# Another way to split 64-bit weights, and another clock model in the planner, in a recurrence-plus-feed-forward kernel

## The chip, the cores and the metric

The kernel runs on one core of one Trainium2 chip. The metric is the device time of one execution in microseconds; the figure before is the median of three executions. The engines are called by the profile's names: PE (TensorE matmuls), PEld (TensorE weight loads), DVE (VectorE), ACT (ScalarE), POOL (GpSimd), SP (SyncE, which issues all DMAs here).

## The reference

The first half is a recurrence over 768 tokens for 4 batches of 8 heads of 40 channels; the second is a gated feed-forward layer with d_ff 1536 on its 3072 x 320 result:

```python
for t in range(S):
    y[:, :, t] = np.einsum('bhd,bhde->bhe', rt, state)
    Sa = np.einsum('bhde,bhe->bhd', state, at)
    state_decay = state * wt[:, :, None, :] - np.einsum('bhd,bhe->bhde', Sa, bt)
    state = state_decay + np.einsum('bhd,bhe->bhde', vt, kt)
...
a = x @ w_a
b = x @ w_b
return (a * b @ w_out).astype(np.float32)
```

The three weight matrices are handed over in 64-bit floating point; everything else is float32.

## The kernel before, in words

**The recurrence** is computed in 12 chunks of 64 tokens, each in two halves `c`. For each half `prep` (line 639) loads the inputs, forms running products with scans on DVE, scales B, K and A, and has PE form the score blocks. `lanes` (line 752) inverts triangular blocks for a group of one or two chunks, in many small DVE steps (tiles `Y`, `Yt`), `join` (807) and `merge` (846) put the blocks together with 32-wide matmuls, and `main` (906) carries the state: PE matmuls, with copies on ACT (`RH`, `SV`, `uT`, `SD`) and products on DVE (`G`, `X`, `ST`) in between. Chunk n+1 needs the state of chunk n. What `main` leaves goes to DRAM (`x_d`), and `pack` (1037) loads it back as the moving operand of the feed-forward layer (`XF`, `xk`).

**The feed-forward layer** is cut into 12 tiles of 128 columns of d_ff. `unit` (510) is one tile against one chunk (256 tokens, tile `ab`) or, in the last third, against two chunks (512 tokens, tiles `at` and `m`): 16 matmuls, a copy on ACT, a product on DVE, a split into high and low part on ACT and on DVE or POOL, and 6 or 12 matmuls into `po`. Tiles 0 to 4 are decoded early, and their units run between the chunks of the recurrence. Two more tiles are decoded around the end of the recurrence and the other five after it.

**Decoding.** Every tile has three pieces (of `wa` and `wb`, 120 partitions x 384, and of `wo`, 128 x 320), 36 pieces in all. `decode` (427) turns one piece, loaded as pairs of 32-bit words, into a high and a low float32 part. It is a list of steps, each with its engine, its planned time and what it reads and writes. There is one set of the temporaries `w_ex`, `w_mt`, `w_rs` (`NTMP` = 1, line 38) and two raw buffers `wraw`. The steps before: the exponent bits of the high word are masked out on DVE; ACT rescales them (a Relu with scale 8 and a bias tile); DVE shifts and masks the mantissa; ACT turns the low word into a float; DVE puts the sign to the exponent, then mantissa to exponent; ACT casts that into the high part; DVE multiplies the low word's float by the signed exponent; a subtraction and an addition (DVE in the first three pieces, POOL in the others) make the low part.

**The order.** Nothing is run in the order of the program text. All steps are given to a planner (`Plan`, line 114), which simulates the engines with the planned times that each step carries, picks at each point the step that can start first (those within `slack` of it by their priority `v`), and emits the instructions in that order; `InOrder` (62) holds every engine to it. So each planned time has a say in the order of all engines. `us` (410) and `act` (416) are the formulas of a DVE and an ACT step of n elements; a PE step has a literal time, and a `work`, which the class `Clock` (95) sums over stretches of time to decide whether PE is taken to run at its full or its slow clock; `switch` (161) is added when PE passes from one kind of block to another. In the decode steps, the priorities `wv`, `PV`, `LV`, `UV` and the others are constants at the head of the file.

```python
def us(n, fixed=0.16, each=0.00106):
    return fixed + each * n
...
def act(n):
    return us(n, 0.17, 0.00088)
```

Of the kernel before, what the change touches and what calls it, by code (L numbers as in the profile page):

```python
# [9 lines left out]
F32 = mybir.dt.float32  # L10
# [42 lines left out]

PV, PV1, LV, MV, UV, WV, WV1 = -2.63, 0.52, -0.08, -0.82, 1.93, -0.57, 0.99
# [40 lines left out]
class Clock:  # L95

    WINDOW, ENOUGH, SLOW = 3.413, 5100, 1.85

    def __init__(self):
        self.work = {}  # L100

    def full(self, t):
        return self.work.get(int(t / self.WINDOW) - 1, 0.0) >= self.ENOUGH

    def run(self, t, d, work):

        left = 1.0
        while left > 1e-9:
            k = int(t / self.WINDOW)
            d1 = d if self.full(t) else d * self.SLOW  # L110
            part = min(left, ((k + 1) * self.WINDOW - t + 1e-9) / d1)
            self.work[k] = self.work.get(k, 0.0) + part * work
            t += part * d1
            left -= part
        return t


class Plan:
# [9 lines left out]
    def op(self, eng, dur, fn, r=(), w=(), v=None, lat=0.07, need=None, free=(), mode=None, moved=0.0, work=0, port=False):  # L128
        o = Op()
        o.moved, o.work, o.port = moved, work, port or (eng == "POOL" and dur != 1.2)  # L130
        o.eng, o.dur, o.fn, o.lat, o.need, o.free, o.mode = eng, dur, fn, lat, need, free, mode
        o.v = self.v if v is None else v
        o.pairs = PAIRS.get(fn.__name__, 8 if work in (3840, 7680) else 0) if eng == "PE" else 0
# [12 lines left out]
        return o  # L146
# [14 lines left out]
    def run(self, slack=0.05, switch=0.13):  # L161
# [17 lines left out]
        while todo:  # L179
# [31 lines left out]
            if o.eng == "PE":  # L211
                if o.mode != last_mode:
                    d += switch
                last_mode = o.mode
                if CLK:
                    t = engines["PE"]
                    if self.filler and s - t > 0.4:

                        share = FILL if clock.full(t) else FILLC
                        nf = int(share * (s - t) / (0.09 if clock.full(t) else 0.17))  # L220
                        for _ in range(nf):
                            self.filler()
                            t = clock.run(t, 0.09, 384)
                        self.nfill = getattr(self, "nfill", 0) + nf
                        s = max(s, t)
# [107 lines left out]
def wkv_moe(ctx, tc, wd, ai, bk, rvf, vn, pin, rv, wa, wb, wo, out):  # L333
# [60 lines left out]
    bias = const.tile([P, 1], F32, name="bias")  # L394
    nc.gpsimd.memset(bias, -8.0 * 0x38000000)
# [31 lines left out]
    def decode(i, src, rows, ncol, dst_hi, dst_lo, split):  # L427
# [10 lines left out]
        if not WIDE:  # L438
# [6 lines left out]
        rf, f = rs.bitcast(F32), mt.bitcast(F32)  # L445
# [4 lines left out]
        yield "DVE", us(ncol), lambda: ts(  # L450
            out=ex, in0=high, scalar1=0x7FF00000, scalar2=None, op0=ALU.bitwise_and), (kr,), (K[0],), None
        yield "ACT", act(ncol), lambda: nc.scalar.activation(
            out=ex, in_=ex, func=AF.Relu, scale=8.0, bias=bias[:rows]), (), (K[0],), None
        yield "DVE", us(ncol), lambda: ts(
            out=mt, in0=high, scalar1=3, scalar2=0x007FFFF8, op0=ALU.logical_shift_left, op1=ALU.bitwise_and), (kr,), (K[1],), None
# [3 lines left out]
        yield "DVE", us(ncol), lambda: stt(  # L459
            out=ex, in0=high, scalar=-2147483648, in1=ex, op0=ALU.bitwise_and, op1=ALU.bitwise_or), (kr,), (K[0],), None  # L460
        yield "DVE", us(ncol), lambda: nc.vector.tensor_tensor(out=mt, in0=ex, in1=mt, op=ALU.bitwise_or), (K[0],), (K[1],), None
# [48 lines left out]
    def unit(xk, kx, w, slot, first, last, done, v, wide=False, quick=False):  # L510
# [29 lines left out]
        for j in range(2):  # L540
            pl.op("PE", 1.81 if wide else 0.95, lambda j=j: half(j), list(kx) + wk, [kab], v=v, work=3840 * scale, mode="r", lat=0.1)
# [16 lines left out]
        def second2():  # L558
            second()

        pl.op("PE", 1.77 if wide else 0.9, second2 if wide else second, km[1:3] + [("wt", slot, 2), ("wh", slot, 2)], kpo,
              v=v - 0.2, work=3840 * scale, mode="r", lat=0.1)
# [76 lines left out]
    def prep(n, c, v):  # L639
# [67 lines left out]
        pl.op("PE", 1.15, scores, [kBK, kA], need=ps, work=4096, mode="q", lat=0.1, w=[("sc", q), kAB, kTK])  # L707
# [27 lines left out]
        for k in range(2):  # L735
            ps = Banks(1)

            def nat(k=k, ps=ps):
                for m in range(4):
                    transp(bank(ps)[:, m * P:(m + 1) * P], BK[:, k * 4 + m].rearrange("p x t -> p (x t)"))  # L740

            def natc(k=k, ps=ps):
                nc.scalar.copy(out=BN[:, k * 4:(k + 1) * 4], in_=bank(ps).rearrange("p (m j e) -> p m j e", m=4, j=2)[..., 0:D])
            pl.op("PE", 0.42, nat, [kBK], need=ps, work=832, mode="t", lat=0.1, w=[("nt", q, k), (*kBN, k)])
            pl.op("ACT", act(320), natc, [("nt", q, k)], [(*kBN, k)], free=[(ps, 0)])
# [61 lines left out]
    def join(n, x, v):  # L807
# [11 lines left out]
        pl.op("PE", 2.55, xt, [("EO", place[n]), ("T3", x)], [("j1", n), "W4"], need=ps, work=3072, mode="h", lat=0.1)  # L819
# [15 lines left out]
        pl.op("PE", 1.15, t3, ["W4", ("TC", x)], [("j2", n), ("T3", x)], need=ps, work=1024, mode="h", lat=0.1)  # L835
# [6 lines left out]
        pl.op("PE", 2.3, tc_, ["W4", ("j2", n)], [("j3", n), ("TC", x)], need=ps2, work=2048, mode="h", lat=0.1)  # L842
# [3 lines left out]
    def merge(n, x, v):  # L846
# [25 lines left out]
        pl.op("PE", 1.15, l2a, kab + [("T3", x)], [("l3", n), "W4"], need=ps, work=1024, mode="h", lat=0.1)  # L872
# [13 lines left out]
        pl.op("PE", 1.15, l2b, ["W4", ("TC", x)], [("l4", n), kT[2]], need=ps, work=1024, mode="h", lat=0.1)  # L886
# [19 lines left out]
    def main(n, c, v):  # L906
# [32 lines left out]
        pl.op("PE", 1.05, r_, [kS, kV, kU], [("r", q), kRH], need=ps, work=2560, mode="c", lat=0.1)  # L939
# [15 lines left out]
        pl.op("PE", 1.1, u_, [kRH, *kT], [("u", q), kS, ("ut", 0), ("ut", 1)], need=ps, work=3328, mode="q", lat=0.1)  # L955
# [9 lines left out]
        if n < NS - 1:  # L965

            ps = Banks(1)

            def s_(ps=ps):
                for i in range(4):  # L970
                    for gq in range(2):
                        for j in range(2):
                            c0 = (i * 2 + gq) * D
                            mul(bank(ps)[hd(j), c0:c0 + D], BN[:, mi(gq, i), j], SV[:, gq, j, i])
            pl.op("PE", 0.75, s_, [kU, kS, kV], [("s", q), kST], need=ps, work=2560, mode="c", lat=0.1)
# [19 lines left out]
        pl.op("PE", 1.15, g_, [("ut", 0), ("ut", 1), kRV], [("gs", q), ("gm", 0), ("gm", 1)], need=ps, work=4096, mode="q", lat=0.1, v=v + 0.1)  # L995
# [17 lines left out]
        pl.op("PE", 1.6, y_, [("gm", 0), ("gm", 1), kU, kRV, kSD], [("y", q), ("x", 0)], need=ps, work=6144, mode="c", lat=0.1, v=v + 0.1)  # L1013
# [8 lines left out]
        if n < NS - 1:  # L1022
# [6 lines left out]
            pl.op("PE", 0.45, sd_, [kST], [("sd_", q), kSD], need=ps, work=832, mode="t", lat=0.1, v=v + 0.3)  # L1029
# [421 lines left out]
```

## Time and profile before

| | |
|---|---|
| three executions | 789.76, 791.24, 792.59 us; median 791.24 us |
| the profiled execution's own time | 793.49 us |
| its span, first to last instruction | 791.8 us |
| busy in the span | PE 693.2, PEld 627.2, DVE 581.8, ACT 403.4, POOL 182.8 us |
| mean granted clock of PE | 0.898 of full speed |

The profiled execution took 2.25 us more than the median of the three; 1.7 us of its time lie outside its span. The page gives busy time by engine, 40 slices of about 20 us, and the chain of work that ended last; the trace behind it gives the same for any stretch.

### The profile page before, as it was taken

What the parts mean: (1) busy time and instruction counts of PE and PEld (TensorE: products, weight loads), DVE (VectorE), ACT (ScalarE), POOL (GpSimd) and SP (SyncE); (2) the same over time, 40 slices, a digit from 0 to 9 for tenths busy, and PEclk for the clock granted to TensorE, in tenths of its full rate; (3) what the DMA queues carried; (4) which work ended last, traced back from release to release, by engine and by line L of the source; (5) the groups of instructions that cost most, each with busy time, mean ns of one, the idle gap of its engine ahead of it and who ended that gap; (6) DMA issues with size and microseconds to landing.
All of it is one profiled execution on the core that took longest, in us unless ns stands there. A gap on an engine that the chain in (4) does not pass through costs nothing.

```text
span 791.8 us, 29711 instructions
## 1 busy us (share of the span) xinstructions
PE 693.2 (88%) x12869; PEld 627.2 (79%) x12869; DVE 581.8 (73%) x1120; ACT 403.4 (51%) x997; POOL 182.8 (23%) x201
## 2 busy tenths in 40 slices
PE   5436748899679998998999899999999999999996
PEld 3436647798579898988888798989988888888885
DVE  8779887679988997998899984873677786232243
ACT  4438638646566476556646447764644443222221
POOL 5000203200120111102012011442635455221220
PEclk9555655789789998998999799999999999999999
DMA  6879887587977778787876467857321210000013
GB/s 196 245 221 275 261 237 208 152 236 210 253 236 234 219 223 240 240 245 189 250 238 173 130 210 208 249 142 232 106 69 41 59 51 13 1 1 1 1 73 132
DMA packets 99479, 132.55 MB, mean 167 GB/s; under 512 B 28524, under 2 KB 75596, under 8 KB 96524
## 3 DMA queue, kind: packets, MB, share of 16 engines
q1 hardware_dynamic: 99340, 130.56, 56.0%
q8 instruction: 103, 1.69, 0.9%
q14 instruction: 36, 0.29, 0.1%
HBM read 87.45 MB, written 38.43 MB: 159 GB/s over the span
## 4 chain that ended last, share of the span: by engine, by line
PE 70%; DVE 11%; DMA 7%; issue 5%; SPq 2%; ACT 2%; POOL 1%; DVEq 0%; ACTq 0%; POOLq 0%
PE at L72 41%; PE ab L72 18%; PE po L72 10%; SPq L72 2%; DMA XF<-x_d 2%; DVE Yt L72 2%; DVE Y L72 2%; DMA A<-in_ai_dram 1%; DMA un<-un_d 1%; DMA BK<-in_bk_dram 1%; DVE G L72 1%; DVE BK L72 1%; DVE Q L72 1%; DMA SV<-in_vn_dram 1%; DMA W<-in_wd_dram 1%
## 5 line engine op out<-in xcount | busy, mean ns | idle before, releaser
L72 PE MATMUL at<-xk,wt 120*128 120x512 f32 x640 | 154.2, 393 | 0.0
L72 PE MATMUL ab<-xk,wt 120*128 120x256 f32 x1024 | 145.5, 295 | 1.7 <-issue 1.7
L72 PEld LDWEIGHTS at<-xk,wt 120*128 120x128 f32 x640 | 118.4, 188 | 23.9
L72 PEld LDWEIGHTS ab<-xk,wt 120*128 120x128 f32 x1024 | 134.1, 199 | 4.0 <-issue 1.8
L72 POOL TENSOR_TENSOR gl<-g,gh 128x256 fp32r<-128x256 f32 x54 | 44.9, 833 | 254.8 <-ACT gh L72 232.8
L72 DVE TENSOR_TENSOR m<-at,m 128x512 f32<-128x512 f32 x40 | 27.6, 690 | 92.5 <-PE at L72 91.6
L72 POOL TENSOR_TENSOR m<-m,m 128x512 fp32r<-128x512 f32 x39 | 51.0, 1307 | 116.3 <-ACT m L72 116.3
L72 PE MATMUL po<-wo,gh 128*128 128x320 f32 x256 | 69.6, 325 | 0.0
L72 DVE TENSOR_TENSOR Y<-Y,Yt 128x31 f32<-128x31 f32 (+20 forms) x185 | 64.2, 347 | 6.3
L72 DVE TENSOR_TENSOR Yt<-Y,N 128x31 f32<-128x31 f32 (+20 forms) x185 | 62.6, 338 | 4.1
L72 PE MATMUL at<-SV,un 128*64 128x40 f32 (+1 forms) x1472 | 52.1, 234 | 15.0 <-DMA SV<-in_vn_dram 8.2
L72 PEld LDWEIGHTS at<-SV,un 128*64 128x64 f32 (+1 forms) x1472 | 46.4, 145 | 21.7 <-issue 15.4
L72 ACT CAST m<-m 128x512 fp32r<-128x512 f32 x40 | 24.8, 621 | 70.1 <-DVE m L72 59.0
L72 PE MATMUL at<-A,BK 64*64 64x64 f32 x1536 | 35.4, 254 | 22.4 <-DVE A L72 12.3
L72 PEld LDWEIGHTS at<-A,BK 64*64 64x64 f32 x1536 | 31.6, 165 | 25.4 <-issue 15.4
L72 ACT COPY m<-at 128x512 f32<-128x512 f32 x40 | 23.3, 583 | 49.6 <-PE at L72 49.3
L72 PEld LDWEIGHTS po<-wo,gh 128*128 128x128 f32 x256 | 45.9, 191 | 1.6
L72 ACT COPY g<-ab 128x256 f32<-128x256 f32 x64 | 23.8, 374 | 45.3 <-PE ab L72 43.9
L72 DVE TENSOR_TENSOR g<-ab,g 128x256 f32<-128x256 f32 x64 | 26.6, 416 | 26.9 <-ACT g L72 26.6
L72 POOL TENSOR_TENSOR w_mt<-w_mt,wt 120x384 f32<-120x384 f32 x22 | 22.5, 1025 | 96.3 <-ACT wt L72 90.6
L72 PE MATMUL po<-wo,m 128*128 128x320 f32 x240 | 42.1, 310 | 2.0 <-DVE m L72 1.3
L72 PEld LDWEIGHTS po<-wo,m 128*128 128x128 f32 x240 | 38.4, 188 | 5.4 <-DVE m L72 1.5
(120 smaller groups left out, 1488.7 us busy)
## 6 DMA issues: line engine op xcount, KB each, us to landing
un<-un_d SPq DMA_DIRECT2D x22, 1092.0 KB
BK<-in_bk_dram SPq DMA_DIRECT2D x22, 448.0 KB
rv<-in_rvf_dram SPq DMA_DIRECT2D x22, 448.0 KB
un_d<-bkn SPq DMA_DIRECT2D x22, 320.0 KB
x_d<-X SPq DMA_DIRECT2D x24, 256.0 KB
un_d<-pe SPq DMA_DIRECT2D x22, 260.0 KB
un_d<-A SPq DMA_DIRECT2D x44, 128.0 KB
un_d<-TK SPq DMA_DIRECT2D x44, 128.0 KB
```

The costliest lines, as they stand in the source:

```text
L72: r = fn(*args, **kwargs)
```

## The change

The decode steps of a piece, the class `Clock`, the planned times and `work` of most PE blocks and the default of `switch` are others; a branch of the planner that is never taken before (its `filler` is always `None`) is gone, and so are the bias tile and its memset. In the decode: ACT scales the high word, read as a float, by a constant and takes the sign of it (two steps); DVE shifts the high word and flips one bit; ACT turns the low word into a float as before and takes the absolute value of the shifted word; DVE multiplies by the sign, and then masks the exponent and sign out of the product; the cast, the multiplication of the low part, the subtraction and the addition are as before.

```diff
+SMALLEST = 0.5 / (1.125 * 2.0 ** -15)
...
-    WINDOW, ENOUGH, SLOW = 3.413, 5100, 1.85
+    WINDOW, FIRST, KEEP, LIFT, SLOW = 3.4133, 1.37, 2560, 2820, 1.75
...
     def full(self, t):
-        return self.work.get(int(t / self.WINDOW) - 1, 0.0) >= self.ENOUGH
+
+        k = int((t - self.FIRST) / self.WINDOW + 1)
+        if k <= 0:
+            return True
+        if k not in self.state:
+            was = self.full(t - self.WINDOW)
+            self.state[k] = self.work.get(k - 1, 0.0) >= (self.KEEP if was else self.LIFT)
+        return self.state[k]
...
-            k = int(t / self.WINDOW)
+            k = int((t - self.FIRST) / self.WINDOW + 1)
             d1 = d if self.full(t) else d * self.SLOW
-            part = min(left, ((k + 1) * self.WINDOW - t + 1e-9) / d1)
+            part = min(left, (k * self.WINDOW + self.FIRST - t + 1e-9) / d1)
...
-    def run(self, slack=0.05, switch=0.13):
+    def run(self, slack=0.05, switch=0.0):
...
-    bias = const.tile([P, 1], F32, name="bias")
-    nc.gpsimd.memset(bias, -8.0 * 0x38000000)
...
-        rf, f = rs.bitcast(F32), mt.bitcast(F32)
+        rf, f, sg = rs.bitcast(F32), mt.bitcast(F32), ex.bitcast(F32)
...
-        yield "DVE", us(ncol), lambda: ts(
-            out=ex, in0=high, scalar1=0x7FF00000, scalar2=None, op0=ALU.bitwise_and), (kr,), (K[0],), None
         yield "ACT", act(ncol), lambda: nc.scalar.activation(
-            out=ex, in_=ex, func=AF.Relu, scale=8.0, bias=bias[:rows]), (), (K[0],), None
-        yield "DVE", us(ncol), lambda: ts(
-            out=mt, in0=high, scalar1=3, scalar2=0x007FFFF8, op0=ALU.logical_shift_left, op1=ALU.bitwise_and), (kr,), (K[1],), None
+            out=ex, in_=high.bitcast(F32), func=AF.Copy, scale=SMALLEST), (kr,), (K[0],), None
+        yield "ACT", act(ncol), lambda: nc.scalar.activation(out=sg, in_=ex, func=AF.Sign), (), (K[0],), None
+        yield "DVE", us(ncol, 0.15, 0.0005), lambda: ts(
+            out=mt, in0=high, scalar1=3, scalar2=0x40000000, op0=ALU.logical_shift_left, op1=ALU.bitwise_xor), (kr,), (K[1],), None
 
         yield "ACT", act(ncol), lambda: nc.scalar.activation(
             out=rf, in_=low.bitcast(U32), func=AF.Copy, scale=2.0 ** -52), (kr,), (K[2],), None
-        yield "DVE", us(ncol), lambda: stt(
-            out=ex, in0=high, scalar=-2147483648, in1=ex, op0=ALU.bitwise_and, op1=ALU.bitwise_or), (kr,), (K[0],), None
-        yield "DVE", us(ncol), lambda: nc.vector.tensor_tensor(out=mt, in0=ex, in1=mt, op=ALU.bitwise_or), (K[0],), (K[1],), None
+        yield "ACT", act(ncol), lambda: nc.scalar.activation(out=f, in_=f, func=AF.Abs), (), (K[1],), None
+        yield "DVE", us(ncol), lambda: nc.vector.tensor_mul(out=f, in0=f, in1=sg), (K[0],), (K[1],), None
+        yield "DVE", us(ncol, 0.15, 0.0005), lambda: ts(
+            out=ex, in0=mt, scalar1=-8388608, scalar2=None, op0=ALU.bitwise_and), (K[1],), (K[0],), None
...
-            pl.op("PE", 1.81 if wide else 0.95, lambda j=j: half(j), list(kx) + wk, [kab], v=v, work=3840 * scale, mode="r", lat=0.1)
+            pl.op("PE", 1.81 if wide else 0.96, lambda j=j: half(j), list(kx) + wk, [kab], v=v, work=1920 * scale, mode="r", lat=0.1)
...
-        pl.op("PE", 2.55, xt, [("EO", place[n]), ("T3", x)], [("j1", n), "W4"], need=ps, work=3072, mode="h", lat=0.1)
+        pl.op("PE", 1.85, xt, [("EO", place[n]), ("T3", x)], [("j1", n), "W4"], need=ps, work=1536, mode="h", lat=0.1)
...
-        pl.op("PE", 2.3, tc_, ["W4", ("j2", n)], [("j3", n), ("TC", x)], need=ps2, work=2048, mode="h", lat=0.1)
+        pl.op("PE", 1.25, tc_, ["W4", ("j2", n)], [("j3", n), ("TC", x)], need=ps2, work=1024, mode="h", lat=0.1)
...
-        pl.op("PE", 1.15, g_, [("ut", 0), ("ut", 1), kRV], [("gs", q), ("gm", 0), ("gm", 1)], need=ps, work=4096, mode="q", lat=0.1, v=v + 0.1)
+        pl.op("PE", 1.09, g_, [("ut", 0), ("ut", 1), kRV], [("gs", q), ("gm", 0), ("gm", 1)], need=ps, work=1280, mode="q", lat=0.1, v=v + 0.1)
```

The other PE blocks are changed in the same way: planned times by 0.01 to 0.15 us (the score block from 1.15 to 1.06), and `work` halved, or cut a little further for the transposes (832 to 338).

## Rows read from the trace of the kernel before

**Rows 1.** The page: engines' busy time, and 40 slices of the span in tenths

```profile
PE 693.2 (88%) x12869; PEld 627.2 (79%) x12869; DVE 581.8 (73%) x1120; ACT 403.4 (51%) x997; POOL 182.8 (23%) x201
PE   5436748899679998998999899999999999999996
DVE  8779887679988997998899984873677786232243
PEclk9555655789789998998999799999999999999999
```

**Rows 2.** Windows: stretch, length, busy PE, PEld, DVE, ACT, POOL, PEclk, DMA

```profile
55.00:240.00 185.00, 139.29 (x4211) 126.89 (x4210) 156.83 (x304) 116.44 (x293) 27.60 (x28) 0.71 0.79 228
240.00:480.00 240.00, 227.30 (x5656) 210.95 (x5654) 209.00 (x438) 139.32 (x379) 30.16 (x38) 0.95 0.73 214
480.00:540.00 60.00, 57.47 (x1151) 54.19 (x1142) 43.58 (x83) 40.48 (x103) 22.08 (x24) 1.00 0.70 203
560.00:680.00 120.00, 120.00 (x644) 106.13 (x643) 85.39 (x141) 53.03 (x103) 58.98 (x53) 1.00 0.18 51
```

**Rows 3.** Windows of tile w_ex alone: stretch, length, DVE, ACT, PEclk, DMA

```profile
55.00:240.00 185.00, 30.20 (x60) 8.99 (x15) 0.71 0.79 228
480.00:540.00 60.00, 16.98 (x30) 4.82 (x8) 1.00 0.70 203
560.00:680.00 120.00, 38.12 (x54) 7.70 (x13) 1.00 0.18 51
```

**Rows 4.** Decode on DVE, 55 to 240 us, by form: count, busy, mean ns

```profile
L72 DVE TENSOR_TENSOR w_rs<-w_rs,w_ex 120x384 f32<-120x384 f32 x10 | 6.4, 637 | 0.2 <-ACT w_rs L72 0.2
L72 DVE TENSOR_TENSOR w_mt<-w_ex,w_mt 120x384 int32<-120x384 int32 x10 | 5.6, 558 | 0.3
L72 DVE SCALAR_TENSOR_TENSOR w_ex<-wraw,w_ex 120x384 int32<-120x384 int32 x10 | 5.5, 548 | 0.2
L72 DVE TENSOR_SCALAR w_ex<-wraw 120x384 int32<-120x384 int32 x10 | 4.4, 444 | 0.5 <-DMA wraw<-in_wa_dram 0.4
L72 DVE TENSOR_SCALAR w_mt<-wraw 120x384 int32<-120x384 int32 x10 | 3.5, 355 | 2.6 <-POOL wt L72 1.8 <-POOL wo L72 0.8
...
L72 DVE SCALAR_TENSOR_TENSOR w_ex<-wraw,w_ex 128x320 int32<-128x320 int32 x5 | 2.4, 487 | 1.9 <-ACT w_ex L72 1.9
```

**Rows 5.** Decode on ACT, 55 to 240 us, by form

```profile
L72 ACT ACTIVATE w_ex<-w_ex,bias 120x384 int32<-120x384 int32 x10 | 6.2, 619 | 1.6 <-DVE w_ex L72 1.5
L72 ACT CAST wt<-w_mt 120x384 fp32r<-120x384 f32 x10 | 5.1, 508 | 3.9 <-DVE w_mt L72 3.8
L72 ACT ACTIVATE w_rs<-wraw 120x384 f32<-120x384 uint32 x9 | 5.1, 564 | 0.3
```

**Rows 6.** The chain that ended last, decode's shift-and-sign pieces: start, us

```profile
56.89 0.46 DVE w_ex L72
...
62.22 0.48 DVE w_ex L72
...
67.26 0.41 DVE w_ex L72
...
90.41 0.41 DVE w_ex L72
```

**Rows 7.** What PE waited for, 55 to 240 us: us in total, times, longest

```profile
PE at L72 <- issue: 18.9, 16, 2.8
PE at L72 <- DVE T L72: 8.9, 2, 5.6
PE at L72 <- ACT T L72: 3.2, 1, 3.2
PE at L72 <- ACT TC L72: 3.1, 1, 3.1
PE at L72 <- ACT W L72: 2.9, 2, 2.4
```

**Rows 8.** Windows of 20 us: ACT is the fourth busy time

```profile
60.00:80.00 20.00, 13.23 (x460) 12.31 (x457) 19.22 (x32) 16.83 (x37) 1.37 (x2) 0.50 0.91 275
120.00:140.00 20.00, 16.99 (x610) 15.45 (x604) 16.16 (x25) 17.81 (x39) 7.03 (x6) 0.50 0.71 207
```

**Rows 9.** Timeline of PE: two score blocks, one 32-wide block: start, us

```profile
57.79 1.98 PE L72 MATMUL at<-A,BK 64*64 64x64 f32 x64 [2.42 <-ACT W L72]
61.51 1.93 PE L72 MATMUL at<-TC,W 32*32 32x32 f32 x126
331.91 1.11 PE L72 MATMUL at<-A,BK 64*64 64x64 f32 x64
```

**Rows 10.** The chain that ended last: its two longest transfers after 55 us

```profile
198.81 7.38 DMA un<-un_d
507.74 7.75 DMA XF<-x_d
```

**Rows 11.** Groups of instructions on ACT, whole span: the table load

```profile
L72 ACT ACT_TABLE_LOAD x1 | 1.3, 1283 | 0.8 <-PEq L1440 0.8
```

More of the change, by code (lines that the diff above doesn't have):

```diff
@@ L95 @@
 class Clock:
-    WINDOW, ENOUGH, SLOW = 3.413, 5100, 1.85
+    WINDOW, FIRST, KEEP, LIFT, SLOW = 3.4133, 1.37, 2560, 2820, 1.75
     def __init__(self):
-        self.work = {}
+        self.work, self.state = {}, {}
     def full(self, t):
-        return self.work.get(int(t / self.WINDOW) - 1, 0.0) >= self.ENOUGH
+        k = int((t - self.FIRST) / self.WINDOW + 1)
[5 more added lines that the diff above has]
+        return self.state[k]
     def run(self, t, d, work):
@@ L132, in op @@
         o.v = self.v if v is None else v
-        o.pairs = PAIRS.get(fn.__name__, 8 if work in (3840, 7680) else 0) if eng == "PE" else 0
+        o.pairs = PAIRS.get(fn.__name__, 8 if work in (1920, 3840) else 0) if eng == "PE" else 0
         o.deps, o.users, o.end, o.ready, o.seq = set(), [], None, 0.0, len(self.ops)
@@ L215, in run @@
                 if CLK:
[L216 to L225, printed above, removed]
                     d = clock.run(s, d, o.work) - s
@@ L559, in second2 @@
             second()
-        pl.op("PE", 1.77 if wide else 0.9, second2 if wide else second, km[1:3] + [("wt", slot, 2), ("wh", slot, 2)], kpo,
-              v=v - 0.2, work=3840 * scale, mode="r", lat=0.1)
+        pl.op("PE", 1.77 if wide else 0.89, second2 if wide else second, km[1:3] + [("wt", slot, 2), ("wh", slot, 2)], kpo,
+              v=v - 0.2, work=1920 * scale, mode="r", lat=0.1)
         if last:
@@ L706, in scores @@
                             mul(bank(ps, kind)[half(j ^ kind), c0:c0 + C], BK[r, m, gq ^ kind], A[r, m])
-        pl.op("PE", 1.15, scores, [kBK, kA], need=ps, work=4096, mode="q", lat=0.1, w=[("sc", q), kAB, kTK])
+        pl.op("PE", 1.06, scores, [kBK, kA], need=ps, work=2048, mode="q", lat=0.1, w=[("sc", q), kAB, kTK])
         def ab(ps=ps):
@@ L743, in natc @@
                 nc.scalar.copy(out=BN[:, k * 4:(k + 1) * 4], in_=bank(ps).rearrange("p (m j e) -> p m j e", m=4, j=2)[..., 0:D])
-            pl.op("PE", 0.42, nat, [kBK], need=ps, work=832, mode="t", lat=0.1, w=[("nt", q, k), (*kBN, k)])
+            pl.op("PE", 0.4, nat, [kBK], need=ps, work=338, mode="t", lat=0.1, w=[("nt", q, k), (*kBN, k)])
             pl.op("ACT", act(320), natc, [("nt", q, k)], [(*kBN, k)], free=[(ps, 0)])
@@ L834, in tc_ @@
                     mul(bank(ps)[r, cm * HB:(cm + 1) * HB], XT[r, cm], TC[r, x, cm])
-        pl.op("PE", 1.15, t3, ["W4", ("TC", x)], [("j2", n), ("T3", x)], need=ps, work=1024, mode="h", lat=0.1)
+        pl.op("PE", 1, t3, ["W4", ("TC", x)], [("j2", n), ("T3", x)], need=ps, work=512, mode="h", lat=0.1)
         def t3c(ps=ps):
@@ L871, in l2a @@
                     mul(bank(ps)[p1:p1 + HB, cm * HB:(cm + 1) * HB], S[p0:p0 + HB, cm, HB:], T3[p0:p0 + HB, x, cm])
-        pl.op("PE", 1.15, l2a, kab + [("T3", x)], [("l3", n), "W4"], need=ps, work=1024, mode="h", lat=0.1)
+        pl.op("PE", 1.13, l2a, kab + [("T3", x)], [("l3", n), "W4"], need=ps, work=512, mode="h", lat=0.1)
         def w4(ps=ps):
@@ L885, in l2b @@
                     mul(bank(ps)[p0:p0 + HB, cm * HB:(cm + 1) * HB], W4[p1:p1 + HB, cm], TC[p1:p1 + HB, x, cm])
-        pl.op("PE", 1.15, l2b, ["W4", ("TC", x)], [("l4", n), kT[2]], need=ps, work=1024, mode="h", lat=0.1)
+        pl.op("PE", 1.13, l2b, ["W4", ("TC", x)], [("l4", n), kT[2]], need=ps, work=512, mode="h", lat=0.1)
         def tb(ps=ps):
@@ L938, in r_ @@
                         mul(bank(ps)[half(j), k:k + D], AK[:, gq, j, i], SV[:, gq, j, i])
-        pl.op("PE", 1.05, r_, [kS, kV, kU], [("r", q), kRH], need=ps, work=2560, mode="c", lat=0.1)
+        pl.op("PE", 1.06, r_, [kS, kV, kU], [("r", q), kRH], need=ps, work=1280, mode="c", lat=0.1)
         pl.op("ACT", act(320), lambda ps=ps: nc.scalar.mul(
@@ L954, in u_ @@
                                 mul(bank(ps, j)[half(gq), i * D:(i + 1) * D], T[h, m], RH[h, m, 0:D])
-        pl.op("PE", 1.1, u_, [kRH, *kT], [("u", q), kS, ("ut", 0), ("ut", 1)], need=ps, work=3328, mode="q", lat=0.1)
+        pl.op("PE", 1, u_, [kRH, *kT], [("u", q), kS, ("ut", 0), ("ut", 1)], need=ps, work=1664, mode="q", lat=0.1)
         for j in range(2):
@@ L974, in s_ @@
                             mul(bank(ps)[hd(j), c0:c0 + D], BN[:, mi(gq, i), j], SV[:, gq, j, i])
-            pl.op("PE", 0.75, s_, [kU, kS, kV], [("s", q), kST], need=ps, work=2560, mode="c", lat=0.1)
+            pl.op("PE", 0.74, s_, [kU, kS, kV], [("s", q), kST], need=ps, work=1280, mode="c", lat=0.1)
             sv = ST[:, :, :, 0:D]
@@ L1012, in y_ @@
                         mul(bank(ps, gq)[hd(j), i * C:(i + 1) * C], BN[:, mi(gq, i), j], G[:, gq, j, i], not n, True)
-        pl.op("PE", 1.6, y_, [("gm", 0), ("gm", 1), kU, kRV, kSD], [("y", q), ("x", 0)], need=ps, work=6144, mode="c", lat=0.1, v=v + 0.1)
+        pl.op("PE", 1.61, y_, [("gm", 0), ("gm", 1), kU, kRV, kSD], [("y", q), ("x", 0)], need=ps, work=3072, mode="c", lat=0.1, v=v + 0.1)
         X, kX = X_[0], ("x", 0)
@@ L1028, in sd_ @@
                     transp(bank(ps)[:, i * P:(i + 1) * P], ST[:, i].rearrange("p q d -> p (q d)"))
-            pl.op("PE", 0.45, sd_, [kST], [("sd_", q), kSD], need=ps, work=832, mode="t", lat=0.1, v=v + 0.3)
+            pl.op("PE", 0.4, sd_, [kST], [("sd_", q), kSD], need=ps, work=338, mode="t", lat=0.1, v=v + 0.3)
             pl.op("ACT", act(320), lambda ps=ps: nc.scalar.copy(
```

## The prediction, on record before the result

> **What bounds the kernel now.** I read the page first: PE is busy for 88% of the span, but the slices show two different kernels [rows 1]. In the last 13 slices PE is full and its clock is full; in the first 12 it is neither, while DVE stands at 6 to 9 tenths. The windows put numbers to that [rows 2]: from 55 to 240 us PE is busy for 139.3 of 185.0 us and its granted clock is 0.71, with DVE at 156.8 us (85%); from 240 to 480 us PE is busy for 95%; from 480 to 540 us for 57.5 of 60; from 560 to 680 us for 120.0 of 120. So the end of the kernel is set by how early the PE work of the first 240 us gets done, and after that by PE's own work, which the change leaves alone.
>
> The clock is two levels, 1.2 and 2.4 GHz; a mean of 0.71 says that some 58% of the stretch (107 us) was at the lower one. What that costs is read from one block at both: 64 matmuls of scores took 1.98 us early and 1.11 us later [rows 9], a factor of 1.78.
>
> Then the windows of the decode's tile [rows 3]: of the 36 pieces (by ACT's rescaling step) 15 lie between 55 and 240 us, 8 between 480 and 540, and 13 between 560 and 680 us. Nothing of the decode runs before 55 us, so the first 55 us are not touched by the edit of the steps, only by the new order.
>
> **The decode on DVE, first stretch.** Two tensor-scalar steps, a scalar-tensor-tensor, an OR and a product become two tensor-scalar steps and two products. The pairs: shift for shift (355 ns), OR for sign product (558 ns for 384 columns, both read two tensors of SBUF), the low product stays (637 ns), and the exponent mask over every second word (444 ns) becomes a mask over adjacent words. For that last one the nearest rows are the two tensor-scalar rows, 355 to 444 ns; I take 444, so no gain from it, with 10 x 0.09 = 0.9 us left for the range [rows 4]. What goes is the scalar-tensor-tensor: 10 x 0.548 + 5 x 0.487 = 7.9 us of DVE [rows 4]. How much of it is on the path? The chain of waits holds four of these 15 instructions, 0.46 + 0.48 + 0.41 + 0.41 = 1.8 us [rows 6]. That is one bound, 7.9 us is the other (DVE is 85% busy there, so a step that is gone often lets a later one begin earlier), and nothing is the floor if the cover is the DMA queue. I take 3 us, nearer to the chain than to the sum, because most of the chain in this stretch is not decode.
>
> The way through one piece gets shorter as well: mask, rescale, scalar-tensor-tensor, OR, cast is 0.444 + 0.619 + 0.548 + 0.558 + 0.508 = 2.68 us; scale, sign, product, cast is 0.564 + 0.508 + 0.558 + 0.508 = 2.14 us [rows 4, 5], with one hand-over between DVE and ACT less. This frees the single set of temporaries earlier; I count nothing for it beside the 3 us.
>
> **The decode on ACT, first stretch.** The rescaling with a bias (619 ns) is replaced by a scaling that reads every second word (nearest row: the low word's, 564 ns), a sign and an absolute value. Those two are not in the trace; bounds are the cast (508 ns) and the step with a bias (619 ns), and I take the cast, which has no bias either [rows 5]. Per piece of 384 columns 0.564 + 0.508 + 0.508 - 0.619 = 0.96 us more, up to 1.2; for 15 pieces, the narrower ones taken like the others, 14.4 us, up to 18. ACT is busy for 116.4 of 185 us there [rows 2], so it has the room on the whole, at 131. It does not have it everywhere: in two windows of 20 us it stands at 16.8 and 17.8 us [rows 8]. PE's listed waits for ACT's `T`, `TC` and `W` sum to 9.2 us [rows 7]; behind a longer decode step on ACT's queue wait just such copies out of PSUM, and PE behind them. I take 1 us of loss; the bounds are 0 and 14.4.
>
> **The later pieces.** Between 480 and 540 us PE is idle for 2.5 us in all [rows 2]; 8 pieces take 8 x 0.96 = 7.7 us more on ACT, busy for 40.5 of 60 us, and some 8 x 0.55 = 4.4 us less on DVE, busy for 43.6. Their units come much later than the decode. I count 0, between -2 (all of the idle time) and +4 (half of ACT's extra). From 560 to 680 us PE is busy for the whole 120 us, while ACT has 53.0 and DVE 85.4 us [rows 2]; 13 pieces add 12.5 us to ACT and take 7 off DVE. The cover is PE's own queue of units over tiles already decoded; were a weight tile late, PE would stand still for the rest of its decode, some 2 us a piece. I count 0. The memset of the bias tile is too small to be a term.
>
> **The new order.** All planned times enter the order of every engine, so this is the least certain term. The new times are nearer to the rows. A `tc_` block of 128 small matmuls had 2.3 us, at the slow clock 2.3 x 1.85 = 4.3; now 1.25 x 1.75 = 2.2, and 126 of them took 1.93 us at the slow clock [rows 9]. A tensor-scalar of 384 columns was planned at 0.16 + 0.00106 x 384 = 0.57 us and is now 0.34, against a row of 0.355 [rows 4]. A planner that sees DVE free sooner and PE faster hands out work closer to when it can run. What there is to win is PE's idle time in the stretch, 185.0 - 139.3 = 45.7 us, less the 18.9 us that it spent on issue, which no order of mine removes [rows 2, 7]: 26.8 us, and some of the slow clock with it. What there is to lose is a wait like those on the two longest transfers after 55 us, 7.4 and 7.8 us [rows 10]: 0 to 12 us, should one of them become worse and PE have nothing else at hand. I take a gain of 8 us, three tenths of the 26.8.
>
> **The sum.** -3 + 1 + 0 - 8 = -10 us, against the profiled execution's own 793.5 us: 783.5. That execution was 2.25 us above the median of the three, so on the median I say 781. Ends: a gain of 7.9 + 0.9 on DVE and 17 from the order gives 791 - 26 = 765; the slower rival below gives 803.
>
> **Rivals.** First, **ACT's queue takes over, slower**. Place: 60 to 140 us, where ACT is at 84 and 89% in two windows [rows 8] and each piece puts 0.96 us more in front of the copies that PE waits for. Price: all of the 14.4 us that do not fit into ACT's idle time, less the 3 us from DVE, so up to +11.4 and more likely +6: 795 to 803. It decides when PE's waits for ACT in this stretch grow from the 9.2 us listed to over 18. For it: those two windows, and that the copies are in the state's own circle. Against: over the whole stretch ACT has 68.6 us idle [rows 2].
>
> Second, **nothing measurable, 789 to 793**: decode is in the shadow. Eleven of the 15 scalar-tensor-tensor steps are not on the chain [rows 6], the issue waits stay, and the new order wins as often as it loses. For it: PE is 95% busy from 240 us on and takes the next unit anyway.
>
> Third, **the order alone makes it slower, over 803**, by moving a load of the state's inputs or of `XF` behind others on SP's queue, with two waits of some 7.5 us [rows 10]. It asks for both in one stretch without PE work at hand.
>
> Fourth, **sign and copy exchange the tables of ACT**. The trace has one table load, 1.28 us, for all functions that the kernel uses [rows 11]. If each piece brought two more, 15 x 2 x 1.28 = 38 us would come to ACT in the first stretch, 131 + 38 = 169 of 185 us, and half of it to the end: 810. The Trainium skill (ScalarE: Activation LUTs, section "Table sets: the hidden batching unit") says that cheap functions such as relu, copy, identity and abs are filler in every set, but does not name sign there, and that a change of set costs about 2.7 us with the drain. With that figure it would be, as an estimate from that page, 80 us of ACT; the one load of this trace agrees with its 1.28 us share, and shows nothing of sign.
>
> Fifth, **the order wins much more**, under 765, by also bringing the clock up before 140 us: at a factor of 1.78, each 10 us of slow PE work that becomes fast gives 4.4 us.
>
> **Chances.** The forecast's case (765 to 788, centre 781) 0.52; much faster 0.06; nothing measurable 0.14; ACT's queue 0.22; order alone slower 0.04; tables 0.02. About 0.3%, or 2.4 us, is what a measurement can tell here: faster 0.52 + 0.06 = 0.58, same 0.14, slower 0.22 + 0.04 + 0.02 = 0.28. The range 765 to 803 leaves out 0.06 below and 0.06 above. Cases of both signs hold much of the chance; the likeliest one's own range is 765 to 788.
>
> **What would show it.** Right: in the changed profile DVE has 36 instructions fewer in decode and ACT 72 more, one table load; between 55 and 240 us DVE's busy time is some 8 us lower, ACT's some 14 us higher, PE's idle time under 38 us, and the slices with a full PE begin earlier by about 10 us. The stretch after 560 us keeps its length. Wrong: PE's waits for ACT before 240 us doubled (first rival); more than one table load (fourth); or PE idle after 240 us grown by more than 5 us, which would say that the order gave back later what the decode won.

## The result, and the profile after

The changed kernel takes 800.25 us in the median of four executions (799.39 to 800.87); the kernel before, run beside it, 790.5 us (789.64 to 792.59). The ratio is 1.0119, with an interval of 1.0095 to 1.0142: slower by some 9.5 us, where 781 was forecast. The profiled execution took 800.37 us, with a span of 798.7 us against 791.8: this pair is 6.9 us apart, somewhat less than the medians. In what follows a median is that of all executions of a kernel, while the ratios leave out executions more than 1.5% above its fastest, so the two need not match.

The page of the kernel after: busy time by engine, and its slices in tenths, the counterpart of [rows 1].

```profile
PE 695.1 (87%) x12869; PEld 628.5 (79%) x12869; DVE 559.1 (70%) x1084; ACT 432.2 (54%) x1069; POOL 186.0 (23%) x200
...
PE   5447647789869999899999999999999999999996
...
DVE  8788797879779896778989996377565555222243
...
PEclk8555757779759999999999999899999999999998
```

The edit did what its text says: DVE has 36 instructions fewer and 22.7 us less to do, ACT 72 more and 28.8 us more. PE has the same 12869 matmuls; its busy time grew by 1.9 us and its idle time by 5.0, together the 6.9 us between the two spans. So most of the loss in this pair is waiting, and the windows tell where to look, with the columns of [rows 2]:

```profile
55.00:240.00 185.00, 136.37 (x4193) 124.12 (x4180) 149.87 (x280) 122.20 (x308) 26.35 (x28) 0.69 0.74 218
240.00:480.00 240.00, 226.43 (x5590) 209.14 (x5589) 207.50 (x438) 139.90 (x380) 33.55 (x40) 0.99 0.72 218
480.00:540.00 60.00, 55.61 (x1287) 51.62 (x1287) 35.97 (x66) 41.87 (x108) 16.95 (x18) 0.94 0.61 177
560.00:680.00 120.00, 120.00 (x656) 107.18 (x655) 70.37 (x131) 67.34 (x139) 62.17 (x56) 1.00 0.27 77
```

PE's idle time from 55 to 240 us went from 45.7 to 48.6 us, and from 240 to 540 us from 15.2 to 18.0. From 560 to 680 us there is none in either kernel, and from there to the end 7.7 and 7.6 us. DVE is 7.0 us lighter in the first stretch, and PE got nothing for it.

**Decode itself.** The new steps between 55 and 240 us by form, first DVE, then ACT, to be held against [rows 4, 5]:

```profile
L73 DVE TENSOR_TENSOR w_rs<-w_rs,w_ex 120x384 f32<-120x384 f32 x10 | 5.6, 558 | 0.3
L73 DVE TENSOR_TENSOR w_mt<-w_mt,w_ex 120x384 f32<-120x384 f32 x10 | 5.5, 548 | 2.0 <-ACT w_mt L73 1.9
L73 DVE TENSOR_SCALAR w_mt<-wraw 120x384 int32<-120x384 int32 x10 | 4.0, 400 | 0.1
L73 DVE TENSOR_SCALAR w_ex<-w_mt 120x384 int32<-120x384 int32 x10 | 3.6, 358 | 0.2
...
L73 ACT ACTIVATE w_mt<-w_mt 120x384 f32<-120x384 f32 x10 | 5.2, 521 | 2.0 <-DVE w_mt L73 1.9
L73 ACT CAST wt<-w_mt 120x384 fp32r<-120x384 f32 x10 | 5.2, 517 | 0.3 <-DVE w_mt L73 0.2
L73 ACT ACTIVATE w_ex<-wraw 120x384 int32<-120x384 f32 x9 | 5.0, 559 | 0.5 <-DVE w_rs L73 0.4
L73 ACT ACTIVATE w_ex<-w_ex 120x384 f32<-120x384 int32 x9 | 4.7, 523 | 0.3
L73 ACT ACT_TABLE_LOAD x1 | 1.3, 1283 | 0.8 <-PEq L1436 0.8
```

Scale, sign and absolute value cost 559, 523 and 521 ns, less the 619 of the rescaling: 0.98 us a piece, where 0.96 was taken. There is one table load, as before. The last column says what the piece waits for in this kernel: DVE 1.9 us in all for the absolute value. Outside the piece, DVE's step on `TK` stands once for 3.1 us behind ACT's `w_ex`. Per piece, the price of the new steps is as forecast.

**Where the time is.** A chunk's two stores of `X` end its part of the recurrence, so the timeline of the issues `x_d<-X` is a clock for it. The timelines of both kernels around chunk 3 follow: start, duration, engine, what. They show the last store of chunk 2, the input loads of the half that chunk 7 begins with, the DVE products on these inputs, the PE block for `ST` and DVE's first update of it, the first store of chunk 3, and the last store of all. First the kernel before:

```profile
198.31 0.41 SPq L72 DMA_DIRECT2D x_d<-X  x1
199.49 0.44 SPq L72 DMA_DIRECT2D A<-in_ai_dram  x1
...
201.34 0.59 SPq L72 DMA_DIRECT2D BK<-in_bk_dram  x1
...
218.24 1.23 DVE L72 TENSOR_TENSOR BK<-BK,Q 128x1024 f32<-128x1024 f32 x1
218.42 0.81 PE L72 MATMUL at<-SV,un 128*40 128x40 f32 x32 [0.84 <-ACT bkn L72]
219.37 0.50 DVE L72 TENSOR_TENSOR ST<-at,ST 128x320 f32<-128x320 f32 x1
...
223.84 1.49 DVE L72 TENSOR_TENSOR A<-A,pe 128x512 f32<-128x512 f32 x1
...
231.76 0.54 SPq L72 DMA_DIRECT2D x_d<-X  x1
...
526.38 0.41 SPq L72 DMA_DIRECT2D x_d<-X  x1
```

The same of the kernel after, with the PE block that waits for `ST`:

```profile
199.44 0.39 SPq L73 DMA_DIRECT2D x_d<-X  x1
...
220.49 0.38 SPq L73 DMA_DIRECT2D A<-in_ai_dram  x1
...
221.45 0.36 SPq L73 DMA_DIRECT2D BK<-in_bk_dram  x1
...
222.17 0.81 PE L73 MATMUL at<-SV,un 128*40 128x40 f32 x32 [0.89 <-ACT uT L73]
...
225.07 0.69 DVE L73 TENSOR_TENSOR A<-A,pe 128x512 f32<-128x512 f32 x1 [2.39 <-DMA A<-in_ai_dram]
...
227.73 1.23 DVE L73 TENSOR_TENSOR BK<-BK,Q 128x1024 f32<-128x1024 f32 x1 [1.97 <-DMA BK<-in_bk_dram]
...
229.34 0.48 DVE L73 TENSOR_TENSOR ST<-at,ST 128x320 f32<-128x320 f32 x1
...
229.88 0.37 PE L73 MATMUL at<-rv,uT 40*64 40x64 f32 x2 [5.32 <-DVE ST L73]
...
242.04 0.55 SPq L73 DMA_DIRECT2D x_d<-X  x1
...
537.46 0.36 SPq L73 DMA_DIRECT2D x_d<-X  x1
```

Chunk 2 ends 1.1 us later than before. From there to the first store of chunk 3 it took 33.5 us and now takes 42.6: 9.1 us. From there to the last store it is 294.6 and 295.4 us, and from the last store to the end of the span 265.4 and 261.2, so 4.2 us come back there. So the recurrence of this execution is late in one place. The two loads are issued 20 to 21 us later in SP's order than before. Their products stand in DVE's queue ahead of `ST` and each waits some 2 us for its load. The PE block for `ST` began 20.1 us after the end of chunk 2 before and begins 22.7 us after it now; then `ST` followed after 0.1 us before, and after 6.4 us now. These two delays are 8.8 of the 9.1 us, and PE stands still for 5.3 us behind `ST`. Nothing of this is a decode instruction.

Over the whole of that stretch, though, PE is idle no longer than before. With the columns of [rows 2], first before, then after:

```profile
198.31:231.76 33.45, 22.03 (x790) 20.12 (x786) 30.39 (x47) 21.37 (x55) 7.67 (x8) 0.82 0.88 243
199.44:242.04 42.60, 31.52 (x886) 28.88 (x886) 32.01 (x47) 28.64 (x77) 5.93 (x6) 0.68 0.79 221
```

PE's idle time is 11.4 and 11.1 us; it ran 96 more matmuls in the longer stretch, at a granted clock of 0.68 for 0.82. So the recurrence is late by 9.1 us, while PE does other work in part of that time, which fits the 4.2 us that come back after the last store.

PE's waits of the same stretch as [rows 7] show the one for `ST` too:

```profile
PE at L73 <- issue: 31.4, 16, 10.0
PE at L73 <- DVE ST L73: 5.3, 1, 5.3
PE at L73 <- DMA un<-un_d: 2.3, 1, 2.3
```

The entry of 10.0 us looks worse than it is: it lies at 105.4 to 115.4 us, and of the 11 us from 105 to 116 us PE was idle for 8.4 before and is for 10.0 now. Both kernels store the end of chunk 0 at 107.44 us and the end of chunk 2 within 1.1 us. All of PE's waits for ACT in this stretch sum to 13.7 us before and 6.0 after.

### The profile page after: what moved, and what is told of

The parts are those of the page before. It is cut to its first block, busy times and chain, and to the rows that moved or that the text cites. A ratio compares the mean times of both kernels' runs of the same rounds, so it can differ in the third digit from the quotient of the medians.

```text
span 798.7 us, 29757 instructions
## 1 busy us (share of the span) xinstructions
PE 695.1 (87%) x12869; PEld 628.5 (79%) x12869; DVE 559.1 (70%) x1084; ACT 432.2 (54%) x1069; POOL 186.0 (23%) x200
## 4 chain that ended last, share of the span: by engine, by line
PE 64%; DVE 15%; DMA 9%; issue 6%; ACT 3%; SPq 3%; POOL 0%; DVEq 0%; ACTq 0%; POOLq 0%
PE at L73 38%; PE ab L73 15%; PE po L73 10%; SPq L73 3%; DMA un<-un_d 2%; DMA A<-in_ai_dram 2%; DVE Y L73 2%; DVE Yt L73 2%; DMA BK<-in_bk_dram 2%; DVE Q L73 1%; DVE BK L73 1%; DVE A L73 1%; DVE G L73 1%; DMA un_d<-A 1%; DVE pe L73 1%
## 5 line engine op out<-in xcount | busy, mean ns | idle before, releaser
L73 PEld LDWEIGHTS ab<-xk,wt 120*128 120x128 f32 x1024 | 132.1, 196 | 8.3 <-DVE g L73 3.1
L73 POOL TENSOR_TENSOR gl<-g,gh 128x256 fp32r<-128x256 f32 x54 | 46.5, 863 | 237.8 <-ACT gh L73 230.8
L73 PE MATMUL po<-wo,gh 128*128 128x320 f32 x256 | 71.7, 333 | 0.0
L73 DVE TENSOR_TENSOR Y<-Y,Yt 128x31 f32<-128x31 f32 (+20 forms) x185 | 66.7, 361 | 6.4
L73 DVE TENSOR_TENSOR Yt<-Y,N 128x31 f32<-128x31 f32 (+20 forms) x185 | 64.9, 351 | 3.9
L73 POOL TENSOR_TENSOR w_mt<-w_mt,wt 120x384 f32<-120x384 f32 x22 | 25.5, 1161 | 115.1 <-ACT wt L73 66.4
L73 PEld LDWEIGHTS at<-A,BK 64*64 64x64 f32 x1536 | 31.0, 162 | 22.1 <-issue 20.1
L73 PEld LDWEIGHTS po<-wo,m 128*128 128x128 f32 x240 | 39.1, 191 | 5.4 <-DVE m L73 1.5
```

The source lines that it names most:

```text
L73: r = fn(*args, **kwargs)
```

## The experiments

The theory after the result: the new order, drawn by the planner from other planned times, costs the time, and the decode edit costs nothing that can be seen. Rivals: the new steps on ACT do it; or each half of the change does a part. The ratios below are to the kernel before, run beside each kernel, with the 95% interval.

**1. The new decode steps in the old order.** The planner is handed the old list of steps, times and engines; only the instructions differ.

```diff
+        yield "DVE", us(ncol), lambda: nc.scalar.activation(
+            out=ex, in_=high.bitcast(F32), func=AF.Copy, scale=SMALLEST), ...
+        yield "ACT", act(ncol), lambda: nc.scalar.activation(out=sg, in_=ex, func=AF.Sign), ...
+        def signed():
+            nc.scalar.activation(out=f, in_=f, func=AF.Abs)
+            nc.vector.tensor_mul(out=f, in0=f, in1=sg)
+            ts(out=ex, in0=mt, scalar1=-8388608, scalar2=None, op0=ALU.bitwise_and)
```

> The planner and every planned time are those of before, so every engine keeps its order; only the decode's instructions are the changed ones (absolute value, sign product and mask at the place of the OR). Theory 'order' (the changed decode is harmless, the new order loses the time): 785 to 792 us, at or a little under before. Rival 'ACT' (the two further ACT steps a piece hold up the copies that PE waits for): 796 to 802 us, PE's waits for ACT before 240 us doubled.

804.77 us, ratio 1.0173 [1.0087, 1.0259]. DVE's waits from 0 to 240 us (in all, times, longest):

```profile
DVE w_mt L72 <- ACT w_mt L72: 24.1, 15, 3.2
```

All 15 pieces wait, 1.6 us each: this variant puts the absolute value directly ahead of the product, in the slot of the OR, so DVE stands until ACT's queue has come to it. PE's waits for ACT before 240 us, by the same view, are 26.8 us for 14.6 in the kernel before. The time is above both ranges. It measures that slot, and not the change.

**2. The old decode steps in the new order.** The old steps were put into the slots of the new ones.

```diff
+        def signed():
+            stt(out=ex, in0=high, scalar=-2147483648, in1=ex, op0=ALU.bitwise_and, op1=ALU.bitwise_or)
+            nc.vector.tensor_tensor(out=mt, in0=ex, in1=mt, op=ALU.bitwise_or)
...
+        yield "DVE", us(ncol), signed, (K[0],), (K[1],), None
```

> The planner and every planned time are those of the changed kernel, the decode's instructions are those of before. Theory 'order': 799 to 806 us, as slow as the changed kernel or slower by the eight us of DVE that come back. Rival 'ACT': 787 to 793 us.

882.47 us, ratio 1.116 [1.1071, 1.1249]. DVE's waits over the whole span:

```profile
DVE w_ex L73 <- DMA wraw<-in_wo_dram: 41.7, 9, 9.2
DVE w_ex L73 <- DMA wraw<-in_wa_dram: 36.2, 11, 8.5
DVE w_ex L73 <- DMA wraw<-in_wb_dram: 28.4, 8, 5.4
```

The old sign step reads the raw words, and in the slot of the new product it stands behind the next load into that buffer, so it takes its signs from a later piece and waits for the load: 106 us in these rows. The time is far above both ranges and says nothing about the order; the old decode in exactly the new order stays unmeasured.

**3. The new planner alone, and the new decode alone, each planned.** Two kernels, each with one half of the change and an order that its own planner drew: the new `Clock`, PE times and `switch` with the old decode, and the old ones with the new decode. The edits are the two halves of the change's diff.

> The changed Clock, switch and planned PE times with the decode of before, steps and planned times: an order of its own. Theory 'order', if the clock model is to blame: 797 to 805 us. If the order depends on every planned time with no one part to blame: anywhere from 783 to 806 us, and not near the sum of parts. Rival 'ACT': 788 to 793 us.

804.61 us, ratio 1.0189 [1.0107, 1.0271]; its first store of chunk 3 goes at 240.09 us, nearly as late as in the changed kernel, with the old decode.

> The changed decode, steps and planned times, with the Clock, switch and PE times of before: an order of its own. Theory 'order', if the clock model is to blame: 783 to 790 us. If the order is sensitive to any planned time: anywhere from 783 to 806 us. Rival 'ACT': 796 to 802 us.

793.37 us, ratio 1.0017 [0.9973, 1.0061]; first store of chunk 3 at 231.05 us, as in the kernel before, though chunk 2 ended later (203.52 us). Taken by themselves, these two say: planner slower, decode neutral. The next runs showed that one order for each is too few to say that.

**4. The wait for `ST` taken out of the changed kernel.** In the planned order, the PE block that `ST` needs and both `ST` steps are put ahead of the two late products.

```diff
+        st = [o for o in order if tag(o) == (6, "ST")]
+        first = next(o for o in order if tag(o) == (14, "A"))
+        for o in [*st[0].deps, *st]:
+            order.remove(o)
+            i = order.index(first)
...
+            order.insert(i, o)
```

> The changed kernel in its own order but for three steps: the matmuls of the state update of half 0 of chunk 3 and DVE's two steps on tile ST behind them stand ahead of DVE's two products that wait for the loads of A and BK. Theory 'one wait' (DVE's queue stood 4.4 us for those loads with ST behind them, and PE 5.3 us for ST): the output X of that half lands some 6 us earlier than at 242 us, PE's wait for ST goes, and the kernel takes 793 to 796 us. Rival 'many waits' (the new order is late in many places, and another wait takes this one's): X some 2 us earlier at most at the end of chunk 3, time 798 to 801 us.

797.02 us (12 executions, 791.81 to 803.16), between the two ranges; ratio 1.0099 [1.0059, 1.0139]. PE's waits from 195 to 250 us:

```profile
PE at L73 <- ACT bkn L73: 4.2, 1, 4.2
...
PE at L73 <- DVE ST L73: 0.7, 1, 0.7
```

The wait is gone, 5.3 to 0.7 us, and PE has 4.2 us behind `bkn` in its place. Chunk 3 takes 39.1 us in the profiled execution, not 42.6: 3.5 us of 9. (That execution, in the same DVE order up to there, ended chunk 2 at 207.31 us where the changed kernel's ended it at 199.44: the point in time moves by 8 us from execution to execution, and only the length of the stretch is compared.) Against the changed kernel's 1.0119 the time is not resolved. The wait is there, but behind it stands another, and what it costs the whole kernel is not shown.

**5. The old order again, with the absolute value early.** As experiment 1, but the absolute value follows the shift at once.

```diff
+        def shifted():
+            ts(out=mt, in0=high, scalar1=3, scalar2=0x40000000, op0=ALU.logical_shift_left, op1=ALU.bitwise_xor)
+            nc.scalar.activation(out=f, in_=f, func=AF.Abs)
```

> As the run with the changed decode in the order of before, but ACT's absolute value stands right behind the shift, not at the place of the OR. Theory 'order' with a decode that is neutral or better: 783 to 792 us, and DVE's wait for ACT's w_mt (24.1 us before 240 us in the first run) under 6 us. Rival 'ACT': 798 to 805 us again, with PE waiting for ACT's copies.

798.98 us, ratio 1.0088 [1.005, 1.0126]. DVE's waits from 0 to 240 us:

```profile
DVE w_mt L72 <- ACT w_mt L72: 10.2, 7, 2.2
DVE w_mt L72 <- ACT w_ex L72: 5.5, 4, 2.5
```

In an order that was not planned for them, the new steps do cost 0.9% of the time. DVE waits 10.2 us behind the absolute value and 5.5 behind the sign. PE waits longer for ACT too, 25.9 us from 0 to 240 us for 14.6 in the kernel before, as the rival 'ACT' said; the three longest sums:

```profile
PE at L72 <- ACT T L72: 5.0, 2, 3.5
PE at L72 <- ACT bkn L72: 4.1, 5, 1.5
PE at L72 <- ACT TC L72: 3.4, 2, 2.2
```

**6. The same, with the absolute value on DVE.** A tensor-scalar mask in place; ACT keeps scale and sign, and DVE has five steps as before.

```diff
-            nc.scalar.activation(out=f, in_=f, func=AF.Abs)
+            ts(out=mt, in0=mt, scalar1=0x7FFFFFFF, scalar2=None, op0=ALU.bitwise_and)
```

> The order of before with a decode between the two: as the changed one, but the absolute value is a mask on DVE (tensor-scalar, in place, right before the sign product) in place of a step on ACT; ACT has four steps a piece, DVE five. Theory 'hand-over' (in the order of before, the changed decode lost its 7 us because DVE stood for ACT's absolute value and sign: 15.7 us of DVE waits before 240 us): 786 to 793 us, those waits halved. Rival 'order only, the decode's mix does not matter': 795 to 800 us again.

792.86 us, ratio 1.0023 [0.9983, 1.0063]. The same view:

```profile
DVE w_mt L72 <- ACT w_ex L72: 2.7, 4, 1.1
```

No wait for `w_mt` on ACT is left, and PE's waits for ACT fell from 25.9 to 18.3 us. So the absolute value on ACT is the likeliest cost of experiment 5; the two intervals touch, so its size of some 0.65 points is rough. Whether it costs by the trip from DVE to ACT and back or by the longer queue on ACT ahead of PE's copies is not separated here: moving it to DVE ends both, and the two profiled executions took the same time (795.49 and 795.65 us), so their waits put no price on it.

**7. Two planners, one after the other.** The old planned numbers until the planner's 250 us and the new ones from there, and the reverse; the old decode in both.

```diff
+UNTIL, FIRST_NEW = 250, False
...
+                new = (s >= UNTIL) != FIRST_NEW
```

> The decode of before. The planner uses the clock class, the PE times and the switch of before for PE steps that it starts before its own 250 us, and the changed ones from there on; so the first 240 us or so keep the order of before. Theory 'place' (the changed kernel lost its ten us between the ends of chunks 2 and 3, near 200 to 242 us, and what comes after chunk 3 takes as long under either planner): chunk 3's first X near 232 us and 786 to 794 us. Rival 'everywhere' (a new order loses a per cent wherever it is drawn): 795 to 805 us, with chunk 3 as before and the rest later.

792.99 us, ratio 1.0033 [0.9992, 1.0074].

> The other way round: the changed planner up to its 250 us, that of before from there on, decode of before. Theory 'place': chunk 3's first X near 240 us, as in the run with the changed planner alone, and 798 to 806 us. Rival 'everywhere': 793 to 803 us too; the two runs together tell it: if both lose, it is everywhere.

821.47 us, ratio 1.0359 [1.0284, 1.0434]. The first store of chunk 3 and the last store in each, first old then new:

```profile
229.98 0.54 SPq L72 DMA_DIRECT2D x_d<-X  x1
...
523.20 0.39 SPq L72 DMA_DIRECT2D x_d<-X  x1
```

and new then old:

```profile
240.64 0.56 SPq L72 DMA_DIRECT2D x_d<-X  x1
...
560.48 0.43 SPq L72 DMA_DIRECT2D x_d<-X  x1
```

The new numbers after chunk 3 do no harm; before it they bring chunk 3 late again, by the same 9 us (240.64 against 231.76). But the second kernel loses another 25 us after that (319.8 us from chunk 3 to the last store, against 294.6 before), under the old numbers, and is slower than both ranges. Late chunks, then, are not the mark of the new planner.

The length of the stretch from the end of chunk 2 to the first store of chunk 3 repeats with the order: 33.5 to 35.3 us in the five traces that keep the order of before up to there (before, experiments 1, 5 and 6, old then new), 40.8 to 43.2 in the three with the new numbers (after, the new planner alone, new then old), with either decode.

**8. No change but 0.01 us.** To every planned end the planner adds a constant, `MARGIN`. It enters the order alone; no instruction changes.

```diff
-MARGIN, DMARGIN = 0.3, 3.0
+MARGIN, DMARGIN = 0.31, 3.0
```

> The kernel before with the planner's constant MARGIN at 0.31 in place of 0.30, which changes no instruction, only the order. Theory 'any change of the order moves the time by a per cent': more than 4 us away from before, most likely slower, 794 to 806 us. Rival 'the clock model is what costs': within 4 us of before, 786 to 794 us.

> The changed kernel with MARGIN at 0.31. Theory 'any change of the order moves the time by a per cent': more than 4 us away from 800, to either side, 788 to 808 us. Rival 'the clock model is what costs': 797 to 804 us again.

> The kernel before with MARGIN at 0.29; no instruction changes, only the order. Theory 'the order of before is an uncommonly good one, and any new one costs about a per cent': 796 to 808 us, like the 807 at 0.31. Rival 'the changed clock model is what costs': 787 to 794 us, with 0.31 as an outlier.

> The changed kernel with MARGIN at 0.29. Theory 'the order of before is an uncommonly good one': 793 to 806 us, in the same band as the orders of the old clock model. Rival 'the changed clock model is what costs': 798 to 806 us, above all orders of the old model but one.

> The changed decode with the old clock model and PE times, MARGIN at 0.31. Theory 'the order of before is an uncommonly good one': 793 to 806 us. Rival 'the changed clock model is what costs': 787 to 795 us, as the 793 at 0.30.

> As the run at 0.31, with MARGIN at 0.29. Theory 'the order of before is an uncommonly good one': 793 to 806 us. Rival 'the changed clock model is what costs': 787 to 795 us. Either way a candidate for an order better than both kernels', under 788 us.

| planner, decode | 0.29 | 0.30 | 0.31 |
|---|---|---|---|
| old, old (the kernel before) | 1.0129 [1.0056, 1.0201] | 1 | 1.0213 [1.0168, 1.0259] |
| new, new (the kernel after) | 1.0267 [1.0161, 1.0373] | 1.0119 [1.0095, 1.0142] | 1.0095 [1.0058, 1.0132] |
| old, new | 1.0226 [1.0131, 1.0322] | 1.0017 [0.9973, 1.0061] | 1.0237 [1.0188, 1.0286] |
| new, old | | 1.0189 [1.0107, 1.0271] | |

A hundredth of a microsecond either way costs the kernel before 1.3 and 2.1% (802.52 and 806.93 us), as much as the whole change or more. With 0.31 its chunk 3 takes 47.4 us, longer than in the changed kernel; its stores of chunk 2 and 3:

```profile
197.64 0.40 SPq L72 DMA_DIRECT2D x_d<-X  x1
245.01 0.39 SPq L72 DMA_DIRECT2D x_d<-X  x1
```

In the changed kernel 0.31 mends chunk 3 (34.0 us from 201.54 to 235.56), and the time is still 1.0095: that execution loses elsewhere. Of these six runs one lies in the range of the theory (802.52 us) and one in that of the rival (798.69 us, the changed kernel at 0.31); the other four are slower than either range. The nine other orders of the table have a mean of 1.0166, and the means without the kernel before itself are 1.0171 for old with old, 1.0160 for new with new, and 1.0160 for the old planner with the new decode; with it, old with old has 1.0114. None of these differ by more than the orders scatter. The kernel before is the best order of the ten, together with one that equals it; the changed kernel is an ordinary one.

No version of these runs beats both kernels: three equal the kernel before within their intervals (1.0017, 1.0023, 1.0033).

## Why the prediction was wrong

- **The new order, taken at -8 us, failed.** The kernel lost some 9.5 us where the sum gained 10. The decode's share of that was not measured in this order. In the table, kernels with the new and the old decode under the same planner differ by -0.7 to +1.0 points, no more than the orders scatter. With the decode taken at nothing, the new order is worth about +10. The step that failed is the argument that planned times nearer to the rows hand out work closer to when it can run; three tenths of the idle time, as its price, had no row behind it. Nothing here shows such an average gain: the new planner's four plain orders lie at 1.0095 to 1.0267. The 18.9 us of issue waits, which no order was to remove, went to 31.4. In the profiled execution the recurrence is late at chunk 3, but at 0.31 the changed kernel has no late chunk 3 and is not measurably faster, so this place is how one order was late and not what a new order costs. The nine other orders of the table lie 0.2 to 2.7% above the kernel before, 1.66% in the mean: some 13 us would have been the right size for the term, which only these runs could tell. The bounds did have this place in them (a loss of 0 to 12 us through late transfers); it was the value taken between them that had the wrong sign. What none of the rows read could tell is that the order of before was an uncommonly good one. The planner's constants may have been chosen for it; no run shows that.
- **DVE's -3 us**: the steps' sizes were right, 7.0 us less busy time of DVE in the stretch for 8 forecast, but PE's idle time there did not fall. In the fixed order, experiment 5 loses 0.9%; experiment 6, which has five steps on DVE as before and so tests little of this saving, gains nothing resolved (1.0023). "One hand-over less" was wrong: the way over scale and sign has one less, but the absolute value lies between two DVE steps and makes another. In the changed kernel the planner hides it (1.9 us of DVE's time).
- **ACT's +1 us**: 0.98 us a piece was right, 0.96 forecast. Busy time in the stretch rose by 5.8 us only and not by 14, because other work of ACT left the stretch: it has 308 instructions there for 293, where 15 pieces alone bring 30 more (two of these ran before 55 us). The first rival's time, 795 to 803, holds the result by luck, for its mechanism is not there: PE's waits for ACT fell from 13.7 to 6.0 us, where it asked for a doubling. That the stated range holds the result is luck for the same reason. In the order of before, which was not planned for the new steps, the mechanism does show: 14.6 to 25.9 us in experiment 5.
- **The later pieces at nothing**: right from 560 to 680 us, where PE is never idle; from 240 to 540 us PE's idle time rose by 2.7 us, less than the 5 that the prediction gave as its sign of a loss there.
- **The third rival**, the order alone, had the mechanism: late loads in SP's queue with PE held behind them. It asked for over 803 us and two such waits, and had a chance of 0.04; the table shows that a loss of 1% or more was the usual outcome of a redrawn order, seven of nine.
- **Tables**: one load; the fourth rival is out.

One reading was short: the chain before holds a fifth of the steps that go, beside the four of [rows 6], so the lower bound for DVE was 2.2 us and not 1.8. It changes nothing in the sum.

```profile
220.40 0.48 DVE w_ex L72
```

What stays open: what the old decode would take in exactly the new order, and so the decode's share of the 9.5 us to better than a per cent; whether any setting of this planner is better on average (with three or four orders each, differences of a per cent are not seen), and why the order of before, and the two drawn ones that equal it, are better than the rest.

## What to carry to other kernels

Where a list scheduler writes the order, an edit to any planned time is a new draw of the whole order: measure the scatter first, with a change that touches no instruction, and read a result against that scatter and not against the spread of repeated runs. To price an edit of the instructions alone, hold the order fixed, and mind that a step moved to another engine between two steps of the first can make a round trip of waits there, and lengthens the other engine's queue. A good order is worth keeping as a written list, since the next edit of the planner loses it.

## What the runs showed that was not expected

- The same program is less repeatable than three runs suggest: 789.76 to 792.59 us in the first three, 782.98 to 804.48 us in 29 executions on another chip, 26 of them within 1.4%. Gaps of half a per cent needed ten or more executions here, and with that spread (a standard deviation of 0.37% in the 26) the interval of the first result, from four executions each, would be about twice as wide, as an estimate, and still above 1.
- The low product is the same instruction in both kernels, and its mean went from 637 [rows 4] to 558 ns; the tensor-scalar steps of 120 x 384 words lie between 355 and 444 ns in both. What ran beside them was not separated.
- Sign, absolute value, copy with scale, and the kernel's other functions on ACT ran with one table load of 1283 ns in all.
